# Twelve 64-column matmuls behind the second pair's scores, and a tensor_tensor in place of a tensor_scalar

## The chip, the core and the metric

The kernel runs on one core of a Trainium2 chip. The metric is the device time of one execution in microseconds (us), as a median of runs. TensorE (PE in the rows) multiplies matrices and writes to PSUM; VectorE (DVE), ScalarE (ACT) and GpSimd (POOL) work on elements; SyncE (SP) issues the DMA transfers. A matmul has its weights loaded by an instruction of its own (PEld in the rows).

## What is computed

An attention of 4 batches, 8 heads, 576 positions and 64 channels, half of the heads with a local mask of 32 positions and half with a mask of every 32nd position, is followed by four expert networks, each weighted by its share of domain_probs:

```python
def _attn_ref(q, k, v):
    scores = scale * np.matmul(q, k.transpose(0, 1, 3, 2))
    ...
    scores = np.where(masks[None, :, :, :], scores, -1000000000.0)
    scores = scores - np.max(scores, axis=-1, keepdims=True)
    attn = np.exp(scores)
    attn = attn / (np.sum(attn, axis=-1, keepdims=True) + 1e-09)
    return np.matmul(attn, v)

def _moe_ref(x, domain_probs, w1, w2):      # x: 2304 x 512
    p = domain_probs / (domain_probs.sum(-1, keepdims=True) + 1e-09)
    for e in range(4):
        h = np.maximum(x @ w1[e], 0.0)      # 512 x 1024
        out += p[:, e:e + 1] * (h @ w2[e])  # 1024 x 512
```

## The kernel before

**Stages.** Attention runs in 16 pairs (a batch and two heads each; "L" local, "S" strided). A pair's scores are small matmuls into PSUM banks named sc (L627 for L, L616 for S), VectorE adds the mask (L641), takes the maximum (L644) and the sum (L655); the subtraction (L647) and the norm (L659) go to VectorE or GpSimd, the exponential to ScalarE (L651). TensorE turns the weights (L706, L722, L739), they are copied out of PSUM (L526, L528), and products with v follow (L791, L771). The first 384 rows of the result are split into a high part xh (ScalarE, L849) and a low part xl (VectorE, L852), the others are copied to xr (L860, L862). Weights are split in the same way into a, s and w2t (high part L884 on ScalarE, low part L885 on VectorE or GpSimd), and each product is made of three passes, high by high, low by high and high by low. The first 384 rows go through all eight half experts by plain products (L969, L985) from about 18 to 198 us, woven with the rest of attention; after that the other rows go through in two parts by a recursive scheme with seven products in place of eight (L1155), with VectorE, ScalarE and GpSimd making the operands (a, s, ring, T, q).

**What sets the order.** Nothing is written in the order in which it runs. Every step is handed to a planner by `add(engine, duration, function, reads, writes, priority, ...)`, and `Plan.walk` plays the program through: for each engine it takes the step that can start first, with ties by priority, follows PSUM banks, the DMA queue and a model of TensorE's clock, and writes down an order in which the instructions are then issued. The durations are estimates in the code. A step marked "VP" goes to VectorE or GpSimd and one marked "AD" to ScalarE or VectorE, whichever the walk finds done first. A changed estimate can so move other steps and change engines. `fill` puts idle 512-column matmuls of a zero tile wz (L1526) into TensorE's early waits. A table SHIFT changes priorities of single steps by their number. Engines run their own instructions in order; waits are on semaphores, and a PSUM bank that TensorE writes is not read by VectorE before the writes to that bank that stand ahead are done.

**Names that come up.** raw are the loaded weights, 1 MB at a load (L874); prs are the domain probabilities, and `normalize` (L1462 to L1467) makes pr from them: a reduction into psums (L1463), the addition of 1e-9 (L1464), a reciprocal (L1465) and a product (L1466), all on VectorE. The second pair (n == 1) is a strided one; its scores are the 24 matmuls of L616 at about 9 us. q8 is the DMA queue by which an engine's instructions come.

Of the kernel before, what the change touches and what calls it, by code (L numbers as in the profile page):

```python
# [8 lines left out]
F32 = mybir.dt.float32  # L9
# [3 lines left out]
ALU = mybir.AluOpType  # L13
# [5 lines left out]
ZN = 30  # L19
# [371 lines left out]
def attn_moe_kernel(  # L391
# [14 lines left out]
    nc = tc.nc  # L406
    B, H, S, D = 4, 8, 576, 64
    NT, DM = B * S, out.shape[1]
    E, _, F = w1.shape
# [33 lines left out]
    psums = const.tile([P, NTT], F32, name="psums")  # L443
    wz = const.tile([P, 512], BF16, name="wz")
    warm = const.tile([P, 8], F32, name="warm")

    wt = {n: big.tile([P, 2, 2, 256], F32R, name=n) for n in QUART[:3] + ("s3",)}
    wq = {n: (t[:, 0], t[:, 1]) for n, t in wt.items()}
# [41 lines left out]
    KORD = (0, 2, 1, 3)  # L490
    JOIN = 4
    WHOLE = (1,)
    order = [(b, c) for b in range(B) for c in KORD]
    NP = len(order)
    plan = Plan(BANKS, MIX, tc)
# [44 lines left out]
    def plan_pair(n):  # L540
# [56 lines left out]
        for gi, (g0, g1) in enumerate(GRP[kd]):  # L597
# [11 lines left out]
            def scores(keys=keys, gi=gi, g0=g0, g1=g1, v0=0):  # L609
                ss = [bank(x) for x in keys]  # L610
                if kd == "S":
                    for o in range(0, 6 * W, W):
                        for x in range(2):
                            for h in range(2):
                                a = slice(64 * h, 64 * h + 64)
                                nc.tensor.matmul(  # L616
                                    ss[h][64 * x:64 * x + 64, o:o + W], qkv[a, x, o:o + 64],
                                    qkv[a, x, QKS + o:QKS + o + SR], start=True, stop=True)
                    return
                for r in range(3):  # L620
                    for v, s in enumerate(ss, v0):
                        for h in range(2):
                            for i in range(2):
                                a = slice(64 * h, 64 * h + 64)
                                t = QB * (2 * gi + v) + (96 * i + 32 * r if spans else 64 * r + 32 * i)
                                p = 64 * (h ^ v) + 32 * i
                                nc.tensor.matmul(  # L627
                                    s[p:p + 32, r * W:r * W + W], qkv[a, t:t + 32],
                                    qkv[a, t + 193:t + 193 + W], start=True, stop=True)
# [33 lines left out]
            dd = nel / 960 + 0.15  # L663
            vp = (dd, nel * 1.6e-3 + 0.22)
            if kd == "S" and gi == 0:
                add("PE", 0.88, scores, [f"qkS{bf}{i}" for i in range(2)], keys + [f"pmS{bf}{i}" for i in range(2)], z + 3, keys,
                    cols=4 * nel)
            elif n == 0 and gi == 0:
                for i, x in enumerate(keys):
                    add("PE", 0.46, half_scores(scores, x, i), [f"qkL{bf}0" + "ab"[i]], [x, tok], z + 3, x, cols=2 * nel)  # L670
            elif kd == "L":
                add("PE", (0.68, 0.46)[gi], scores, [f"qkL{bf}{gi}"], keys + [tok], z + 3, keys, cols=4 * nel)
# [103 lines left out]
        for gi in range(2):  # L776
# [65 lines left out]
            for (t0, nt, nm) in ((0, TA, "x"), (T0[1], TBS[0], "r1"), (T0[2], TBS[1], "r2")):  # L842
                for sel, cols in cut(t0, nt):
# [3 lines left out]
                    if nm == "x":  # L847
# [5 lines left out]
                                out=cols(xl[c]), in0=src(), in1=cols(xh[c].bitcast(F32)), op=ALU.subtract)  # L853

                        add("ACT", 0.42, xhi, [key], [f"xh{c}{g}"], z + 7.2)
                        add("DVE", 0.44, xlo, [key, f"xh{c}{g}"], [f"xl{c}{g}"], z + 7.4)
                    else:
                        def xraw(e, src=src, cols=cols, nm=nm):
                            if e == "ACT":
# [601 lines left out]

    def normalize():  # L1462
        nc.vector.tensor_reduce(out=psums, in_=prs, op=ALU.add, axis=AX.X)  # L1463
        nc.vector.tensor_scalar_add(out=psums, in0=psums, scalar1=1e-9)  # L1464
        nc.vector.reciprocal(out=psums, in_=psums)  # L1465
        nc.vector.tensor_tensor(  # L1466
            out=pr, in0=prs, in1=psums.unsqueeze(2).to_broadcast([P, NTT, E]), op=ALU.mult)  # L1467
# [5 lines left out]
        if n == 1:  # L1473
            add("POOL", 0.1, lambda: nc.gpsimd.memset(raws[2][:, 0, 0:1], 0.0), ["pmS00"], ["raw20", "raw21"], 0)
    add("SP", 0.4, load_pr, (), ["prs"], 8, xfer=((0.1, 128),))
    add("DVE", 1.0, normalize, ["prs"], ["pr"], ZN)
    key = ("ps", "pr")

    def turn_pr():
# [47 lines left out]

    with tc.manual_schedule():
        nc.vector.memset(wz, 0.0)
        make_identity(nc, ident)  # L1530
        for t in pm["S"]:
            nc.gpsimd.memset(t[:, :, SR + 1:64], 0.0)
# [87 lines left out]
```

## Time and profile before

| | |
|---|---|
| median of 3 runs | 778.45 us (776.25 to 778.79) |
| the profiled execution | 778.49 us |
| its span in the trace | 776.7 us |
| TensorE busy | 765.5 us, 5374 matmuls |
| VectorE busy | 620.8 us |
| ScalarE busy | 385.6 us |
| GpSimd busy | 206.4 us |

The span is what the trace covers, from the first instruction to the last. Busy TensorE time counts pipelined matmuls, so a busy stretch can still run at the lower clock; the granted clock (PEclk, 1.0 for 2.4 GHz and 0.5 for 1.2 GHz) tells that apart. Times in the rows are in us from the span's start.

### The profile page before, as it was taken

Reading aid. Unit: us, or ns where it says so; the run is one execution under the profiler, and the core shown is the slowest. Engines: PE = TensorE matmul, PEld = TensorE weight load, DVE = VectorE, ACT = ScalarE, POOL = GpSimd, SP = SyncE. Lnnn points to the kernel's source line nnn. Section 1 sums busy time; section 2 is a strip of 40 time slices with the busy share of each in tenths; the row PEclk is TensorE's granted clock in tenths of the full one; section 3 lists DMA queues with packets and bytes.
Section 4 is the critical chain, followed back from the end, with each engine's and each line's share of the span. In section 5 each row is a group of like instructions: output and inputs, shape, how many; then the busy total and the mean of one; then the engine's idle time right before and its main releaser. Section 6 shows DMA issues by size and latency. Waiting matters only on the chain.

```text
span 776.7 us, 14119 instructions
## 1 busy us (share of the span) xinstructions
PE 765.5 (99%) x5374; PEld 664.6 (86%) x5377; DVE 620.8 (80%) x1016; ACT 385.6 (50%) x726; POOL 206.4 (27%) x198
## 2 busy tenths in 40 slices
PE   7999999999999999999999999999999999999997
PEld 4788888889989999999999998888888888888886
DVE  6877777798698897889798997758765976599895
ACT  4635544474566375646727654644354344523330
POOL 5412011012131522454373264001000330033250
PEclk9999999999999999999999999999999999999999
DMA  9999999778899798899989838955665697659624
GB/s 321 305 394 380 339 326 353 276 252 327 311 388 343 257 359 288 328 237 350 350 254 275 272 119 221 395 207 220 236 265 198 193 215 288 232 173 247 215 82 162
DMA packets 89630, 212.67 MB, mean 274 GB/s; under 512 B 7071, under 2 KB 33883, under 8 KB 89563
## 3 DMA queue, kind: packets, MB, share of 16 engines
q1 hardware_dynamic: 83659, 201.96, 71.8%
q0 software_dynamic: 5760, 9.70, 7.9%
q8 instruction: 42, 0.69, 0.3%
q10 hardware_dynamic: 144, 0.11, 0.1%
q14 instruction: 25, 0.20, 0.1%
HBM read 138.58 MB, written 73.17 MB: 273 GB/s over the span
## 4 chain that ended last, share of the span: by engine, by line
PE 95%; DVE 2%; DMA 1%; ACT 1%; issue 1%; POOL 0%; DVEq 0%; ACTq 0%
PE mo L1155 26%; PE ps L1155 25%; PE sc L1155 20%; PE mo L985 9%; PE mo L969 9%; PE ps L771 2%; DMA ring<-d27a 1%; PE sc L627 1%; PE ps L739 1%; PE sc L616 1%; PE mo L1526 1%; PE ps L791 0%; ACT q L1207 0%; DVE w2t L885 0%; DVE pmL L641 0%
## 5 line engine op out<-in xcount | busy, mean ns | idle before, releaser
L1155 PE MATMUL sc<-T,ring 128*128 128x448 f32 (+2 forms) x774 | 174.3, 374 | 0.0
L1155 PEld LDWEIGHTS sc<-T,ring 128*128 128x128 f32 x774 | 144.5, 188 | 19.7
L1240 ACT ACTIVATE T<-q 128x512 fp32r<-128x512 f32 (+1 forms) x196 | 112.6, 601 | 69.0 <-PE mo L1155 26.4
L1242 DVE TENSOR_TENSOR T<-q,T 128x512 fp32r<-128x512 f32 (+1 forms) x152 | 104.7, 703 | 15.9 <-ACT T L1240 15.2
L1203 DVE TENSOR_TENSOR q<-ps,v 128x448 f32<-128x448 f32 (+1 forms) x96 | 62.5, 654 | 35.3 <-PE ps L1155 30.9
L1155 PE MATMUL mo<-T,ring 128*128 128x512 f32 (+1 forms) x396 | 90.0, 376 | 0.0
L1207 ACT ACTIVATE q<-q 128x448 f32<-128x448 f32 (+1 forms) x84 | 49.9, 598 | 71.7 <-DVE q L1203 70.8
L1155 PEld LDWEIGHTS mo<-T,ring 128*128 128x128 f32 x396 | 74.3, 188 | 10.3
L1242 POOL TENSOR_TENSOR T<-q,T 128x448 fp32r<-128x448 f32 (+1 forms) x44 | 53.1, 1215 | 91.8 <-ACT T L1240 69.9
L985 PE MATMUL mo<-w2t,hs 128*128 128x512 f32 x288 | 71.2, 397 | 0.0
L1194 ACT ACTIVATE v<-mo 128x448 f32<-128x448 f32 (+1 forms) x96 | 54.5, 567 | 25.7 <-PE mo L1155 25.0
L1352 DVE TENSOR_TENSOR acc<-sc,acc 128x512 f32<-128x512 f32 (+1 forms) x85 | 54.9, 654 | 13.9 <-PE sc L1155 13.1
L1284 POOL TENSOR_TENSOR q<-q,q 128x512 f32<-128x512 f32 (+1 forms) x12 | 15.4, 1284 | 181.5 <-DVE T L1242 164.9
L985 PEld LDWEIGHTS mo<-w2t,hs 128*128 128x128 f32 x288 | 52.7, 188 | 11.0
L1284 DVE TENSOR_TENSOR q<-q,q 128x448 f32<-128x448 f32 (+1 forms) x88 | 58.9, 681 | 2.5 <-POOL T L1242 1.4
L526 ACT ACTIVATE acc<-sc 128x448 f32<-128x448 f32 (+1 forms) x41 | 23.2, 567 | 48.5 <-PE sc L1155 46.9
L969 PE MATMUL mo<-xh,a 128*128 128x384 f32 x192 | 45.7, 341 | 0.0
L1352 DVE TENSOR_TENSOR acc<-mo,acc 128x512 f32<-128x512 f32 (+1 forms) x52 | 34.0, 658 | 14.0 <-PE mo L1155 11.3
L1155 PE MATMUL ps<-T,ring 128*128 128x448 f32 (+1 forms) x180 | 40.8, 375 | 0.5 <-DMA ring<-d27a 0.5
L1155 PEld LDWEIGHTS ps<-T,ring 128*128 128x128 f32 x180 | 33.7, 188 | 5.3 <-DVE acc L1352 0.8
L1155 PE MATMUL ps<-t4h,a 128*128 128x448 f32 (+1 forms) x128 | 35.2, 376 | 0.2 <-DVE q L1203 0.2
L1155 PE MATMUL ps<-t3h,s 128*128 128x448 f32 (+1 forms) x128 | 35.2, 376 | 0.1
(179 smaller groups left out, 1437.6 us busy)
## 6 DMA issues: line engine op xcount, KB each, us to landing
raw<-in_w SPq DMA_DIRECT2D x28, 1024.0 KB, 8.3
qkS<-in_qk_strided SPq DMA_DIRECT2D x16, 329.0 KB, 8.2
vstL<-in_v_local SPq DMA_DIRECT2D x6, 640.0 KB, 9.7
po<-acc POOLq DMA_DIRECT2D x16, 224.0 KB, 7.2
vstS<-in_v_strided SPq DMA_DIRECT2D x8, 384.0 KB, 7.8
a<-d16a SPq DMA_DIRECT2D x6, 512.0 KB, 8.7
ring<-d27a SPq DMA_DIRECT2D x6, 512.0 KB, 6.5
a<-d10a SPq DMA_DIRECT2D x6, 512.0 KB, 4.7
```

Source lines behind the costliest of these rows:

```text
L526: nc.scalar.activation(out=dst(), in_=src(held[key]), func=AF.Copy)
L771: nc.tensor.matmul(oo[hf][64 * h:64 * h + 64, o:o + w], a, pt[r, x, c0:c0 + w], start=True, stop=True)
L969: nc.tensor.matmul(pt[:, 0:TA], w[:, c % 2, (f % 2) * P:(f % 2) * P + P], (xl if i == 1 else xh)[c], start=j == 0, stop=j == 11)
L985: nc.tensor.matmul(pt, ht[f][:, ts], wt[f][:, cs], start=j == 0, stop=j == 11)
L1155: nc.tensor.matmul(pt, a[i == 2][:, j, f * P:f * P + P], skewed(b[i == 1][j], TH)[:, cs], start=bool(first) and n == 0, stop=True, skip_gr ...
L1194: add("ACT", TH / 1200 + 0.18, lambda: nc.scalar.activation(out=late["u"][i][:, 0:TH], in_=held[key][:, 0:TH], func=AF.Copy), [key, "late2 ...
L1203: add("DVE", DD, lambda: nc.vector.tensor_tensor(out=q(), in0=src(), in1=late["u"][i][:, 0:TH], op=ALU.add), [key, f"u{i}", "late2"], [tok ...
L1207: add("ACT", TH / 1200 + 0.2, lambda: nc.scalar.activation(out=q(), in_=q(), func=AF.Relu), ["late2"], [tok], zs)
L1240: add("ACT", TH / 1200 + 0.17, lambda src=src, hi=hi: nc.scalar.activation(out=hi(), in_=src(), func=AF.Copy), [tok, "late2"], [f"T{i}h{j} ...
L1242: add("VP", vp, lambda e, src=src, hi=hi, lo=lo: engine(e).tensor_tensor(out=lo(), in0=src(), in1=hi().bitcast(F32), op=ALU.subtract), [to ...
L1284: add("VP", vp, lambda e, d=d, x=x, y=y: engine(e).tensor_tensor(out=d[0](), in0=x[0](), in1=y[0](), op=ALU.subtract), [x[1], y[1]], [d[1] ...
L1352: add("DVE", DD, lambda av=av, key=key: nc.vector.tensor_tensor(out=av(), in0=held[key][:, 0:TH], in1=av(), op=ALU.add), [key], tok, zd)
```

## The change

Behind the 24 score matmuls of the second pair, twelve matmuls with zero weights wz and 64 columns of wz are written into a free part of the pair's first score bank (columns 324 to 387; nothing reads them). The planner is told of them by a longer duration and more columns for that step. The addition of 1e-9 to the domain sums becomes a tensor_tensor with a tile tiny, set to 1e-9 at the start by VectorE, and its planned duration goes from 1.0 to 0.85 for the four operations; the planned duration of each xl goes from 0.44 to 0.54.

```diff
+    tiny = const.tile([P, NTT], F32, name="tiny")
...
+    PAD = 12
...
+                    for _ in range(PAD if n == 1 else 0):
+                        nc.tensor.matmul(ss[0][:, 6 * W:6 * W + 64], wz[:, 0:P], wz[:, 0:64], start=True, stop=True)
...
-                add("PE", 0.88, scores, [f"qkS{bf}{i}" for i in range(2)], keys + [f"pmS{bf}{i}" for i in range(2)], z + 3, keys,
-                    cols=4 * nel)
+                add("PE", 0.88 + (PAD * 0.03 if n == 1 else 0), scores, [f"qkS{bf}{i}" for i in range(2)], keys + [f"pmS{bf}{i}" for i in range(2)], z + 3, keys,
+                    cols=4 * nel + (PAD * 64 if n == 1 else 0))
...
-                        add("DVE", 0.44, xlo, [key, f"xh{c}{g}"], [f"xl{c}{g}"], z + 7.4)
+                        add("DVE", 0.54, xlo, [key, f"xh{c}{g}"], [f"xl{c}{g}"], z + 7.4)
...
-        nc.vector.tensor_scalar_add(out=psums, in0=psums, scalar1=1e-9)
+        nc.vector.tensor_tensor(out=psums, in0=psums, in1=tiny, op=ALU.add)
...
-    add("DVE", 1.0, normalize, ["prs"], ["pr"], ZN)
+    add("DVE", 0.85, normalize, ["prs"], ["pr"], ZN)
...
         nc.vector.memset(wz, 0.0)
+        nc.vector.memset(tiny, 1e-9)
```

Lines move down by one to five in the changed file (L616 becomes L618, the new matmuls are L622, L1464 becomes L1468). By the programs' lists TensorE gets 24 instructions more (12 loads and 12 matmuls), VectorE goes from 1018 to 1024 operations, GpSimd from 203 to 197, ScalarE from 729 to 730; SyncE keeps its 395.

TensorE at the second pair's scores, at about 9 to 14 us, before:

```order
L1526 MATMUL mo<-wz 128x512
L616 MATMUL sc<-qkS_263 64x54 x24
L706 MATMUL ps<-ident,pmL_269 128x128 x6
L1526 LDWEIGHTS wz
L1526 MATMUL mo<-wz 128x512
L627 MATMUL sc<-qkL_261 32x63 x12
L627 MATMUL sc<-qkL_262 32x63 x12
L791 MATMUL ps<-pTL,vstL_265 64x96 x8
```

and now, with ten of the twelve equal pairs left out:

```order
L1530 MATMUL mo<-wz 128x512
L618 MATMUL sc<-qkS_264 64x54 x24
L622 LDWEIGHTS wz
L622 MATMUL sc<-wz 128x64
...
L622 LDWEIGHTS wz
L622 MATMUL sc<-wz 128x64
L710 MATMUL ps<-ident,pmL_270 128x128 x6
```

The pads stand between the scores and the turning of the first pair's weights. Behind them TensorE's order is the same up to about 38 us, 24 instructions further back.

VectorE around the domain sums, at about 28 to 36 us, before (numbers behind names are buffers):

```order
L659 TENSOR_TENSOR pmS_272<-pmS_272,sm 128x6x54
L885 TENSOR_TENSOR w2t<-raw_226,w2t 128x512
L1463 TENSOR_REDUCE psums<-prs 128x18
L1464 TENSOR_SCALAR psums<-psums 128x18
L1465 RECIPROCAL psums<-psums 128x18
L1466 TENSOR_TENSOR pr<-prs,psums 128x72
L641 TENSOR_TENSOR pmL_269<-sc,both 128x3x63 x2
L885 TENSOR_TENSOR w2t<-raw_226,w2t 128x512 x2
L862 COPY xr_241<-ps 128x6x6x3
L852 TENSOR_TENSOR xl_249<-ps,xh_245 128x6x12x3
L885 TENSOR_TENSOR a_77<-raw_225,a_77 128x512
L852 TENSOR_TENSOR xl_249<-ps,xh_245 128x6x12x3
```

and now:

```order
L889 TENSOR_TENSOR w2t<-raw_227,w2t 128x512
L1467 TENSOR_REDUCE psums<-prs 128x18
L1468 TENSOR_TENSOR psums<-psums,tiny 128x18
L1469 RECIPROCAL psums<-psums 128x18
L1470 TENSOR_TENSOR pr<-prs,psums 128x72
L530 COPY pTS<-ps 128x6x64
L651 TENSOR_TENSOR pmL_270<-pmL_270,mx 128x9x63
L856 TENSOR_TENSOR xl_250<-ps,xh_246 128x6x12x3
L645 TENSOR_TENSOR pmL_271<-sc,both 128x3x63
L889 TENSOR_TENSOR a_78<-raw_226,a_78 128x512
L856 TENSOR_TENSOR xl_250<-ps,xh_246 128x6x12x3
```

The norm of pmS and a w2t have left VectorE here, a copy of pTS and a subtraction of pmL have come, and a mask stands ahead of the a between the two halves of xl.

GpSimd at the same time, before:

```order
L885 TENSOR_TENSOR w2t<-raw_226,w2t 128x512
L647 TENSOR_TENSOR pmL_269<-pmL_269,mx 128x9x63
L885 TENSOR_TENSOR s_80<-raw_225,s_80 128x512
L659 TENSOR_TENSOR pmL_269<-pmL_269,sm 128x9x63
L647 TENSOR_TENSOR pmS_271<-pmS_271,mx 128x12x54
```

and now:

```order
L663 TENSOR_TENSOR pmS_273<-pmS_273,sm 128x6x54
L889 TENSOR_TENSOR w2t<-raw_227,w2t 128x512 x2
L889 TENSOR_TENSOR s_81<-raw_226,s_81 128x512
L889 TENSOR_TENSOR w2t<-raw_227,w2t 128x512
L889 TENSOR_TENSOR a_79<-raw_226,a_79 128x512
```

The low part of s follows two w2t directly, with no subtraction of pmL ahead of it. Further differences of this kind lie on all engines up to about 230 us; on SyncE they lie at about 200 to 230 us only.

## Rows read from the trace of the kernel before

**Rows 1.** The page's head and part 1: busy us (share) xinstructions of each engine.

```profile
span 776.7 us, 14119 instructions
PE 765.5 (99%) x5374; PEld 664.6 (86%) x5377; DVE 620.8 (80%) x1016; ACT 385.6 (50%) x726; POOL 206.4 (27%) x198
```

**Rows 2.** TensorE's waits, whole span: us in total, times, longest.

```profile
PE ps L771 <- issue: 1.4, 1, 1.4
```

**Rows 3.** TensorE's waits from 36.2 us to the end.

```profile
PE mo L969 <- DVE xl L852: 0.5, 1, 0.5
PE ps L1155 <- DMA ring<-d27a: 0.5, 1, 0.5
PE ps L1155 <- DVE q L1203: 0.2, 1, 0.2
```

**Rows 4.** By stretches: length, busy of PE, PEld, DVE, ACT, POOL, PEclk, DMA, GB/s.

```profile
23.00:24.00 1.00, 0.86 (x16) 0.80 (x16) 0.00 (x0) 0.38 (x2) 0.18 (x1) 0.82 1.01 407
24.00:25.00 1.00, 1.00 (x27) 0.56 (x33) 0.60 (x2) 0.75 (x4) 0.00 (x0) 0.50 1.04 407
...
27.00:28.00 1.00, 1.00 (x9) 0.94 (x8) 0.30 (x1) 0.83 (x2) 0.00 (x0) 0.97 1.03 360
```

**Rows 5.** Timeline, TensorE at the standstill: start, us, what, idle before and its end.

```profile
20.54 0.33 PE L969 MATMUL mo<-xl,s 128*128 128x384 f32 x1
...
20.98 0.78 PE L771 MATMUL ps<-pTS,vstS 54*64 54x54 f32 x34
23.14 0.45 PE L771 MATMUL ps<-pTS,vstS 54*64 54x54 f32 x14 [1.38 <-issue]
...
23.92 0.52 PE L969 MATMUL mo<-xl,s 128*128 128x384 f32 x1
```

**Rows 6.** The page's part 3, queue of instructions: packets, MB, share.

```profile
q8 instruction: 42, 0.69, 0.3%
```

**Rows 7.** The DMA view from 20 to 21 us: packets, MB, share by queue.

```profile
q1 hardware_dynamic: 175, 0.34, 109.4%
q8 instruction: 1, 0.02, 10.3%
```

**Rows 8.** Timeline from 10 to 30 us: around the pads' place.

```profile
10.75 0.88 DVE L641 TENSOR_TENSOR pmS<-sc,both 128x324 f32<-128x324 f32 x2
...
10.97 0.85 PE L706 MATMUL ps<-ident,pmL 128*128 128x128 f32 x6 [0.99 <-DVE pmL L659]
...
11.55 0.10 PEld L1526 LDWEIGHTS <-wz 128*128 128x128 bf16 x1
...
13.62 0.88 PE L791 MATMUL ps<-pTL,vstL 128*64 128x96 f32 x16 [0.79 <-ACT pmS L651]
...
15.72 0.38 SPq L874 DMA_DIRECT2D raw<-in_w  x1
...
29.12 0.59 PE L739 MATMUL ps<-ident,pmS 64*128 64x64 f32 x12
```

**Rows 9.** Timeline from 24 to 37 us, VectorE, GpSimd and TensorE in turn.

```profile
24.40 0.55 DVE L852 TENSOR_TENSOR xl<-ps,xh 128x216 fp32r<-128x216 f32 x1 [1.87 <-ACT xr L860]
27.70 0.56 DVE L852 TENSOR_TENSOR xl<-ps,xh 128x384 fp32r<-128x384 f32 x1 [0.96 <-ACT xh L849]
28.58 0.69 DVE L885 TENSOR_TENSOR w2t<-raw,w2t 128x512 fp32r<-128x512 f32 x1
29.44 1.10 DVE L1464 TENSOR_SCALAR psums<-psums 128x18 f32<-128x18 f32 x1
34.43 1.21 DVE L885 TENSOR_TENSOR a<-raw,a 128x512 fp32r<-128x512 f32 x1
...
29.22 1.28 POOL L885 TENSOR_TENSOR w2t<-raw,w2t 128x512 fp32r<-128x512 f32 x1 [2.63 <-issue]
33.95 1.14 POOL L647 TENSOR_TENSOR pmL<-pmL,mx 128x567 f32<-128x567 f32 x1 [3.45 <-DVE mx L644]
35.05 1.73 POOL L885 TENSOR_TENSOR s<-raw,s 128x512 fp32r<-128x512 f32 x1
...
36.16 0.44 PE L969 MATMUL mo<-xl,a 128*128 128x384 f32 x1 [0.52 <-DVE xl L852]
```

## The prediction

> **What bounds the kernel now.** I read the share of the engines first [rows 1]: TensorE is busy for 765.5 of 776.7 us. The end moves only where TensorE stands still or runs at its lower clock. The list of its waits names 1.4 us before matmuls of L771, put down to "issue", which means that the profile shows nothing waited for [rows 2]; from 36.2 us to the end there are three, 1.2 us together [rows 3]. Before about 21 us it waits more, but there VectorE sets the pace and such waits do no harm by themselves. The view by stretches [rows 4] shows a second loss: after the standstill the granted clock falls to 0.50, the 1.2 GHz level, from within the row 23:24 to within the row 27:28. The shares of those two rows (0.36 and 0.06 us at half) and the three microseconds between them make 3.4 us at half speed; a matmul of L969 took 0.52 us there and 0.33 before [rows 5]. Half of 3.4, **1.7 us**, is lost. With the standstill's 1.38 us [rows 5] that is 3.1 us in one place, 0.4% of the time.
>
> The profiled execution took 778.49 us, 1.8 more than its span. The median of the three runs is 778.45, so a sum made against this execution holds against the median. One of the three took 776.25, 2.2 less, about the size of this loss; whether it is this loss the runs do not say. A measurement of this kernel can tell about 0.3% (2.3 us) from no change.
>
> **The standstill.** The instruction queue q8 moved 42 packets with 0.69 MB [rows 6], 16.4 KB each; TensorE has 5374 + 5377 instructions [rows 1], so a packet is 256 of them. One lies in the microsecond from 20 to 21, with the DMA share at about one [rows 7], just before TensorE stops at the 34th of 48 matmuls of L771 [rows 5]. So I read the standstill as code that comes late. Counting 256 TensorE instructions (matmuls, loads, waits) back along the timeline leads into the L791 group at 13.62 [rows 8]. If the packet was asked for there, it moved 7 us later, behind other traffic and after the 1 MB load of raw issued at 15.72 [rows 8].
>
> The Trainium skill, "Runtime: NRT & Kernel Launch", section "Instruction fetch mechanics", says that code is fetched ahead in blocks of 256 instructions and that this is mostly hidden. By that sentence the standstill would have another cause and would stay, which is the second rival below; the row with the packet speaks against it.
>
> **The twelve matmuls.** They stand behind L616 of the second pair, where TensorE waits 0.99 us for VectorE until 10.97 [rows 8]. The trace has no row of their form. Nearest from below: transposes of 64 columns, 12 in 0.59 us (L739). Nearest from above: one load of wz, 0.10 us, if every load stays in the open, 12 x 0.10 = 1.2 us [rows 8]. I take 0.8, nearer the transposes, since loads run beside matmuls. That lies inside the 0.99 us: cost 0, at most 0.25. VectorE's second mask of this pair now waits for them too; it begins at about 11.2 (10.75 and half of 0.88, [rows 8]), late enough for pads of up to 1.2 us.
>
> Their other effect is that everything later in TensorE's program stands 24 instructions further back, so each border between code blocks comes 24 instructions earlier in the work. The place 256 before the standstill moves from L791, which TensorE enters at 13.62 after a 0.79 us wait, to matmuls of L627 ahead of that wait, some 1.2 us sooner and further ahead of the raw load. Bounds for the standstill: nothing left, or 1.6 us (it is met 12 small matmuls, 0.2 us, earlier and the packet is no sooner). I take **0.3 us left, -1.1**, nearer to nothing, because a request that stands in front of raw has less to wait behind. L969 would then fill the time before the row 23:24 in which the clock fell, and I expect it to hold: **-1.7**. Its bounds are 0 and 1.7.
>
> **The domain sums.** The tensor_scalar took 1.10 us for 18 columns, where 512 columns of w2t take 0.69; it ran from 29.44 to just behind the end of GpSimd's w2t (29.22 to 30.50) [rows 9]. As a 0.2 us operation it would give VectorE 0.9. But VectorE's two-input a<-raw,a at 34.43 took 1.21 and ended 0.55 behind GpSimd's 33.95 to 35.09 [rows 9]. So the tensor_tensor, or the two-input pr behind it, can wait for w2t just as long: gain 0 to 0.9. I take 0.3, nearer to none, since GpSimd has two w2t in a row there now. The memset of tiny comes behind that of wz, while VectorE waits for the first scores: 0.
>
> The skill, "SBUF — State Buffer", section "Who interferes with whom", says that a VectorE instruction with two SBUF inputs contends with a GpSimd one that reads SBUF, and the later one waits in full. The a<-raw row agrees. By the rule the swap alone gives VectorE 0, by the plain duration 0.9, and the sum below would be 776.4 or 775.5.
>
> **The new plan.** The changed durations and costs reorder work from about 28 to 230 us; behind that all engines' orders are those of before. On VectorE's way to its last xl the order loses the norm of pmS, a w2t and a copy of xr, and gains a copy of pTS, a subtraction of pmL and a mask. Those are operations of 0.3 to 0.7 us (as w2t and a mask in [rows 8, 9]): three against three, taken as 0, within 0.7. DMA orders change only at some 200 us. The same loads stand ahead of the ring load that TensorE waits 0.5 us for [rows 3]: 0, between -0.5 and +0.7.
>
> **The sum.** TensorE would reach the L969 that now starts at 36.16 behind xl [rows 9] 1.1 + 1.7 = 2.8 us sooner, at 33.4. VectorE's two idle waits before it, 1.87 and 0.96 us [rows 9], are for copies of TensorE's results: the first shrinks by 1.1, the second goes, so xl comes 2.1 sooner, 2.4 with the 0.3 of the sums. TensorE still waits there, and the **2.4 us** of VectorE are what is left: 778.5 - 2.4 = **776.1 us**. From there TensorE is back to back and carries it to the end.
>
> **The rivals.**
> - *The code comes earlier and the clock falls all the same.* For it: the clock fell after this standstill in the one execution that I see, and idle stretches before 17 us did not lower it, so what decides is not in the rows. Then -1.1, of which VectorE gives back 0.3: 777.7.
> - *The change does not do what it says.* The packet moves when the DMA queue lets it, and the pads fill an idle 0.99 us and nothing more. Then 778.5, within 0.5.
> - *VectorE gets late (slower).* GpSimd's low part of s, which came behind pmL at 35.05 [rows 9], now follows w2t directly. If it starts at about 35.0, when ScalarE has its high part, and VectorE's a, now behind a mask that needs TensorE's L627, comes after that, a waits for some 1.3 us (as w2t's 1.28, [rows 9]) and xl ends 1.2 later: 779.7. It decides when VectorE's a comes after 35.0, that is if the standstill stays. And it can repeat: six operations leave GpSimd (203 to 197) for VectorE, at some 0.65 us; with no cover 3.9, 782.4. Against it: TensorE waits for nothing between 37 and 230 us, so there is slack. The middle is 780.3, two thirds of the way being the repeats.
>
> **How the numbers follow.** Forecast (776.1, own range 774.8 to 777.4) 0.55; the clock falls 0.15; no effect 0.12; VectorE late 0.18. Below 776.1 lie half of the first, 0.28, and 0.02 of the second and third with a ring wait that vanishes: faster 0.30. Above 780.8 lie two thirds of the last, since a first lateness tends to be followed by others: slower 0.13. Within 0.3% is the rest, 0.57. For 8 in 10 the range runs from 774.8, the forecast's own low end, to 780.3, which leaves out the worse part of the slow case.
>
> **What would show it.** The standstill in L771 under 0.6 us; a granted clock of 1.0 in every row from 20 to 30; L706 starting at 11.0 or little later with the pads before it; the psums operation at 0.2 us, or at about 1 with a GpSimd operation that ends with it; the L969 behind xl at about 33.8 instead of 36.16; no new TensorE waits from 37 to 230. I am wrong if the packet still comes at 20.6 and the clock falls, or if TensorE waits for VectorE by more than 1 us in the stretch to 190 us.

## The result, and the profile after

The changed kernel takes 783.71 us (783.56 to 784.70, 6 runs) where the kernel before takes 777.34 (776.21 to 778.79, 6 runs with the three known earlier): a ratio of 1.0085, with a 95% interval from 1.0069 to 1.0100. It is slower by 6.4 us. I had forecast 776.1 and at most 780.3.

The first thing to see is that several steps of the forecast came true in the trace and were still worth nothing. The profile of the changed kernel by stretches (length, busy of PE, PEld, DVE, ACT and POOL, granted clock, DMA share, GB/s), which answers to [rows 4]:

```profile
23.00:24.00 1.00, 1.00 (x51) 0.70 (x49) 0.44 (x1) 0.89 (x3) 0.34 (x1) 1.00 1.04 409
24.00:25.00 1.00, 0.96 (x27) 0.69 (x16) 0.95 (x4) 0.56 (x1) 0.13 (x1) 1.00 1.03 387
...
27.00:28.00 1.00, 1.00 (x17) 0.68 (x15) 0.97 (x3) 1.00 (x2) 0.87 (x1) 1.00 0.75 219
```

The clock held at 1.0. The twelve matmuls took 0.52 us in the trace (10.00 to 10.52), inside the wait that was there. The standstill within the group of strided products, 1.38 us in [rows 5], is 0.35 in its row now:

```profile
21.23 0.56 PE L775 MATMUL ps<-pTS,vstS 54*64 54x54 f32 x23
22.14 0.61 PE L775 MATMUL ps<-pTS,vstS 54*64 54x54 f32 x25 [0.35 <-issue]
```

This shorter standstill says little by itself: over all traces of this case it is 0.0 to 1.0 us in the seven with the shift of 24 and 0.5 to 1.4 in the eleven without.

And yet the page's first lines show a span 6.2 us longer, with TensorE busy for 4.6 us more with the twelve matmuls as its only new work [rows 1]:

```profile
span 782.9 us, 14145 instructions
...
PE 770.1 (98%) x5386; PEld 664.5 (85%) x5389; DVE 625.4 (80%) x1022; ACT 385.2 (49%) x727; POOL 197.9 (25%) x192
```

TensorE's waits, which answer to [rows 2, 3]: the one for xl grew from 0.5 to 1.4, the one for ring from 0.5 to 0.9, and "issue" stands in two groups:

```profile
PE mo L973 <- DVE xl L856: 1.4, 1, 1.4
...
PE ps L775 <- issue: 1.2, 2, 0.8
PE ps L1159 <- DMA ring<-d27a: 0.9, 1, 0.9
PE sc L631 <- issue: 0.7, 1, 0.7
```

The 0.8 of L775 lies at 136 us, where TensorE did not stand still before; the 0.7 of L631 lies at 13 us. VectorE and GpSimd on the way to that xl, which answer to [rows 9] (start, duration):

```profile
26.25 1.01 DVE L889 TENSOR_TENSOR w2t<-raw,w2t 128x512 fp32r<-128x512 f32 x1
...
27.43 1.02 DVE L1468 TENSOR_TENSOR psums<-psums,tiny 128x18 f32<-128x18 f32 x1
...
28.78 0.97 DVE L1470 TENSOR_TENSOR pr<-prs,psums 128x72 f32<-128x72 f32 x1
...
34.05 1.78 DVE L889 TENSOR_TENSOR a<-raw,a 128x512 fp32r<-128x512 f32 x1
35.76 0.52 DVE L856 TENSOR_TENSOR xl<-ps,xh 128x216 fp32r<-128x216 f32 x1
...
27.13 2.53 POOL L889 TENSOR_TENSOR w2t<-raw,w2t 128x512 fp32r<-128x512 f32 x2 [0.42 <-POOL pmS L663]
34.02 1.28 POOL L889 TENSOR_TENSOR s<-raw,s 128x512 fp32r<-128x512 f32 x1 [4.36 <-ACT s L888]
```

Before, the last xl had begun at 35.56:

```profile
35.56 0.54 DVE L852 TENSOR_TENSOR xl<-ps,xh 128x216 fp32r<-128x216 f32 x1
```

The two-input operations end behind GpSimd's: psums, pr and a take 1.02, 0.97 and 1.78 us, and xl begins at 35.76, 0.2 later than before. Whatever TensorE won by 30 us is gone there.

That explains the start, not the 4.6 us of busy time. Longer matmuls stand in the large products, behind 198 us. The groups of TensorE by shape (busy us, mean ns of one), first three of the kernel before, then of the changed one:

```profile
L1155 PE MATMUL ps<-b11h,a 128*128 128x512 f32 x64 | 18.4, 389 | 0.0
...
L1155 PE MATMUL ps<-t2h,s 128*128 128x512 f32 x64 | 18.4, 389 | 0.0
...
L1155 PE MATMUL ps<-b11h,a 128*128 128x448 f32 x64 | 16.7, 362 | 0.0
```

```profile
L1159 PE MATMUL sc<-T,ring 128*128 128x512 f32 x378 | 90.9, 389 | 0.0
...
L1159 PE MATMUL ps<-t3h,s 128*128 128x512 f32 x64 | 18.9, 396 | 0.0
L1159 PE MATMUL ps<-b11h,a 128*128 128x512 f32 x64 | 18.8, 396 | 0.0
...
L1159 PE MATMUL mo<-t1h,s 128*128 128x512 f32 x64 | 18.6, 392 | 0.0
...
L1159 PE MATMUL ps<-t2h,s 128*128 128x512 f32 x64 | 18.4, 389 | 0.0
...
L1159 PE MATMUL ps<-b11h,a 128*128 128x448 f32 x64 | 17.0, 366 | 0.0
```

The same instruction with the same shapes takes 395 or 396 ns in place of 389 in the high groups of b11, b21, t3 and t4; not in t2 nor in T by ring. Over these four products with 512 columns (64 matmuls by 5 to 7 ns in each of the high groups, 32 by 6 to 9 in each of the low ones) and 448 columns (3 to 4 ns each) that is 4.0 us; t1 and b22 are longer too, by less (392 and 391 ns), which adds 0.4. (The busy time of before also holds the 1.7 us of the lower clock, so these do not add up to the 4.6.) What sets the four apart is not in the program's order but in its memory. Their weight tiles a11, a12, a22 and s3 are allocated at the low end of SBUF behind the constants, their moving tiles b and t at the high end. The compiled programs, from which these addresses are, place tiles at multiples of 32 bytes, so tiny (72 bytes) takes 96:

```
byte within a partition         before   changed
tiny                                 -      4256
a11 (weights of b11)              4768      4864
T0 / ring0 (one product)   53920/123552  54016/123648
b11h0 (moving)                  153504    153504
s2 / t2h0 (one product)   214944/186272  214944/186272
```

T and ring moved together, s2 and t2 not at all; a11 and b11 moved apart by 96 bytes. No row of the profile before shows an address.

### The profile page after: what moved, and what is told of

The parts are those of the page before. It is cut to its first block, busy times and chain, and to the rows that moved or that the text cites. A ratio compares the mean times of both kernels' runs of the same rounds, so it can differ in the third digit from the quotient of the medians.

```text
span 782.9 us, 14145 instructions
## 1 busy us (share of the span) xinstructions
PE 770.1 (98%) x5386; PEld 664.5 (85%) x5389; DVE 625.4 (80%) x1022; ACT 385.2 (49%) x727; POOL 197.9 (25%) x192
## 4 chain that ended last, share of the span: by engine, by line
PE 94%; DVE 2%; DMA 1%; ACT 1%; issue 1%; POOL 0%; DVEq 0%; POOLq 0%
PE mo L1159 26%; PE ps L1159 26%; PE sc L1159 20%; PE mo L989 9%; PE mo L973 8%; PE ps L775 2%; DMA ring<-d27a 1%; PE sc L631 1%; PE sc L618 1%; PE ps L743 1%; PE mo L1530 1%; DVE xl L856 0%; ACT q L1211 0%; DVE mx L648 0%; DVE a L889 0%
## 5 line engine op out<-in xcount | busy, mean ns | idle before, releaser
L1288 DVE TENSOR_TENSOR q<-q,q 128x448 f32<-128x448 f32 (+1 forms) x88 | 57.3, 663 | 4.0 <-POOL T L1246 2.5
```

Source lines behind the costliest of these rows:

```text
L1288: add("VP", vp, lambda e, d=d, x=x, y=y: engine(e).tensor_tensor(out=d[0](), in0=x[0](), in1=y[0](), op=ALU.subtract), [x[1], y[1]], [d[1] ...
```

## The experiments

Every time stands beside runs of the kernel before on the same chip.

### Where the tiles stand

**A dead tile in tiny's place**, in the kernel before:

```diff
     warm = const.tile([P, 8], F32, name="warm")
+    dead = const.tile([P, 18], F32, name="dead")
```

> The kernel before with one edit: a tile of 18 floats per partition that nothing reads or writes, allocated where tiny stands. Tiles are placed at multiples of 32 bytes, so it takes 96 bytes, and a11, a12, a22, s3, the T and ring tiles move up by 96; the b, t, s1, s2 and s4 tiles at the other end of SBUF stay. Program order and instructions are those of before. Theory A (placement: a product is slower when its stationary and its moving tile no longer stand alike): the 512-column products of b11, b21, t3 and t4 take 395 to 398 ns in place of 389, those with 448 columns 365 to 368 in place of 362, T by ring stays at 389; TensorE busy about 4.6 us more; time 782.0 (781.3 to 782.7). Theory B (the longer matmuls come from the new order, from the twelve added ones or from what other engines do): everything as before, 777.3.

Measured: 781.50 us against 777.31, ratio 1.0065 (1.0041 to 1.0090). A tile that nothing touches costs 4.2 us. The same groups are longer, by the same amounts:

```profile
L1156 PE MATMUL ps<-t3h,s 128*128 128x512 f32 x64 | 18.9, 396 | 0.0
L1156 PE MATMUL ps<-b11h,a 128*128 128x512 f32 x64 | 18.8, 396 | 0.0
```

**Which distance?** Three more shifts: the changed kernel with tiny made 128 bytes wide, the kernel before with a dead tile of 64 bytes, and the kernel before with the tiles at the high end moved by 32.

```diff
-    tiny = const.tile([P, NTT], F32, name="tiny")
+    tiny = const.tile([P, 32], F32, name="tiny")[:, 0:NTT]
```

> The changed kernel with tiny made 32 floats wide (128 bytes; only the first 18 are used), so that everything above it moves by 128 bytes and no longer by 96; all else as changed. Theory A (placement, by the place within 64 or 128 bytes): all 512-column products at 389 ns and 448-column ones at 362 again, TensorE busy about 4.6 us less than in the changed kernel, time 783.7 - 4.6 = 779.1 (778.3 to 779.9): still 1.8 above before, for what the early stretch lost. Theory B: products at 395 as in the changed kernel, 783.7.

Measured: 785.70 us against 777.31, ratio 1.0106 (1.0090 to 1.0123). My first idea, the place within 64 or 128 bytes, fell: b11h stayed at 394 ns. That this is 2.0 us more than the changed kernel took goes with the clock: in three of the four executions the mean granted clock is 0.998, and the profiled one shows where it fell, to 0.50 (the 1.2 GHz level) for 3.4 us from 37.5 us on, just behind a wait of 1.5 us for xl:

```profile
36.90 0.45 PE L973 MATMUL mo<-xl,a 128*128 128x384 f32 x1 [1.49 <-DVE xl L856]
```

```profile
37.00:38.00 1.00, 1.00 (x5) 1.00 (x6) 0.97 (x3) 0.45 (x1) 0.00 (x0) 0.74 1.05 369
38.00:39.00 1.00, 1.00 (x5) 1.00 (x4) 0.97 (x3) 0.53 (x2) 0.00 (x0) 0.50 1.11 389
```

```diff
+    dead = const.tile([P, 16], F32, name="dead")
```

> The kernel before with a dead tile of 16 floats (64 bytes) in the place of tiny. If what counts is the place within 64 bytes: 512-column products of b11, b21, t3 and t4 stay at 389 ns, time 777.3 within 1.3. If it is the place within 128 bytes or more, or the bare fact that two tiles have moved against each other: 395 ns or more, 782. Theory B: 389, 777.3.

Measured: 781.25 us in one run, 394 to 396 ns for the four products. So it is not the place within 64 bytes.

```diff
             tmp["s", i] = p.tile([P, 2, 256], F32, name=f"tmp{i}")
+        p.tile([P, 8], F32, name="dead")
```

> The kernel before with a dead tile of 8 floats (32 bytes) behind the tmp tiles at the other end of SBUF, which moves b11 to t4, s1, s2 and s4 down by 32 bytes, onto multiples of 64; a11, a12, a22, s3, T and ring stay 32 above one. If the two tiles of a product must stand alike within 64 bytes: b11, b21, t3, t4 at 395 ns and t1, t2, b22 (whose s1, s2, s4 move with them) at 389, time about 782. If it is that a stationary tile on a multiple of 64 is bad for a moving one that is not (the case of the changed kernel alone): all at 389, 777.3. Theory B: 389, 777.3.

Measured: 783.42 us in one run, the four products at 395 and 396 ns. Here a11 stayed and b11 moved, in dead96 the other way round: it is the distance that counts and not the place of either tile. It need not be the distance of a matmul's own two tiles alone: t1 and b22, whose two tiles moved together or not at all, take 391 to 393 ns in all these runs (high groups, 512 columns), t2 389 or 390. What the products between which they run have to do with it was not tested. Of the products with 512 columns all distances of before are multiples of 256 (a11 to b11: 581 times 256), which gives the next test:

```diff
+    dead = const.tile([P, 64], F32, name="dead")
```

> The kernel before with a dead tile of 64 floats (256 bytes) where tiny stands. In the kernel before, the two tiles of every product stand apart by a multiple of 256 bytes (a11 and b11 by 148736, T and ring by 0 within 2048), and shifts by 64, 96 and 128 bytes and one by 32 the other way all made them slower. Theory A256 (they must stand apart by a multiple of 256): all 512-column products back at 389 ns, time that of before, 777.3 within 0.9. Theory A-other (the exact distance of before is what is good, or any move of a against b hurts): b11, b21, t3, t4 at 395 ns or more, 781.5.

Measured: 777.08 us against 777.14, ratio 1.0002 (0.9990 to 1.0014). All groups are back, t1 and b22 too:

```profile
L1156 PE MATMUL ps<-t3h,s 128*128 128x512 f32 x64 | 18.4, 389 | 0.0
...
L1156 PE MATMUL ps<-b11h,a 128*128 128x512 f32 x64 | 18.4, 389 | 0.0
```

The same in the changed kernel, with `tiny = const.tile([P, 64], F32, name="tiny")[:, 0:NTT]`:

> The changed kernel with tiny 64 floats wide (256 bytes, 18 floats used). Theory A256: products at 389 and 362 ns again, TensorE busy some 4.6 us less than in the changed kernel, time 783.7 - 4.6 = 779.1 (778.2 to 780.0). What is left above 777.3 is what the changed kernel's trace shows ahead of 250 us: the wait for xl 0.9 longer, a standstill of 1.0 at 136 us, the ring wait 0.4 longer, less the 0.9 by which it led at 34 us. Theory A-other: 783.7 or more.

Measured: 780.99 us against 777.14, ratio 1.0050 (1.0034 to 1.0065), with 389 ns in all these groups. The rest of the slowdown, 3.9 us, is more than the 1.8 that I expected to be left. Part of it is the clock again: four of the six executions have a mean granted clock of 0.997 or 0.998 (780.74 to 782.31), two of 1.0 (779.42 and 780.20), 2.7 above before.

### The new order

The four planning numbers of the changed kernel in the kernel before, without the twelve matmuls and without tiny. Of the four, the two for the twelve matmuls leave every engine's planned order as it was (no run has them alone); the two VectorE durations make the new order.

```diff
-                        add("DVE", 0.44, xlo, ...
+                        add("DVE", 0.54, xlo, ...
...
-    add("DVE", 1.0, normalize, ["prs"], ["pr"], ZN)
+    add("DVE", 0.85, normalize, ["prs"], ["pr"], ZN)
```

> The kernel before with the four planning numbers of the changed kernel and nothing else: order as changed (the cost of the twelve matmuls alone leaves the order as it was, so the two VectorE durations make the difference), no twelve matmuls, no tiny, SBUF as before. Theory R (the new order is dear by itself: VectorE's last xl before TensorE's wait at 36 us comes nearly 3 us later than in the old order, because w2t, pr and a wait for GpSimd and a copy, a subtraction and a mask stand before it): 779.8 to 781.0, with a wait for xl of over 1 us at 34 to 36 us. Theory T (it is dear only together with the twelve matmuls, through the place of the code blocks): 777.2 within 0.8.

Measured: 780.77 us against 776.86, ratio 1.0047 (1.0034 to 1.0060). Estimates in the code, which no instruction uses, cost 3.9 us. The median hides two kinds of execution: 779.39 and 779.98 with a granted clock of 0.999 and 1.0, some 2.8 above before, and 780.77 to 781.49 with 0.997 or 0.998. In the kernel before, run beside it, none of 23 is under 0.999. So some 2.8 of the 3.9 are the order's waits, and the rest goes with a clock that falls more often in this order. TensorE's waits show the same places as the changed kernel:

```profile
PE ps L771 <- issue: 1.7, 2, 1.0
PE mo L969 <- DVE xl L852: 1.5, 1, 1.5
...
PE ps L1155 <- DMA ring<-d27a: 1.1, 1, 1.1
```

Each of the two alone, the first hunk of that diff and then the second:

> The kernel before with the planned duration of the xl subtraction at 0.54 in place of 0.44, nothing else. VectorE then has a mask of the next pair ahead of its last xl there, and a<-raw,a before both, as in the changed kernel, but a copy of xr on VectorE still. Theory R1 (this number brings the dear order): most of what planonly costs, 779 to 781. Theory R2 (it takes both): 777.1 within 0.8.

> The kernel before with the planned duration of normalize at 0.85 in place of 1.0, nothing else. VectorE then does its xl ahead of the maximum of pmL, and the a<-raw,a between the last two xl is gone from VectorE's way. Theory R1 (the xl number brings the dear order): 777.1 within 0.8, or less than before, down to 775.5, where the wait for xl shortens. Theory R3 (this number brings it): 779 to 781.

Measured: 778.25 us (ratio 1.0016, 1.0007 to 1.0024) and 778.38 (1.0021, 1.0013 to 1.0030). Neither brings the dear order alone; both orders are a little worse than the old one.

**What is dear in it?** The order of planonly, with three GpSimd subtractions (two w2t at 27 us, one s at 34 us) replaced by a memset of the same tile:

```diff
+        def low(e):
+            if e == "POOL":
+                gone[0] += 1
+                if gone[0] in (3, 4, 5):
+                    nc.gpsimd.memset(lo().bitcast(F32), 0.0)
+                    return
+            engine(e).tensor_tensor(out=lo(), in0=src(), in1=hi().bitcast(F32), op=ALU.subtract)
```

> The order of planonly, with three GpSimd operations replaced, the two w2t at 27 us and the low part of s at 34 us: each writes zeros over the same tile in place of subtracting (so these low parts are left out of the computation). They then read nothing from SBUF. Theory X (the new order is dear because VectorE's two-input operations there wait for GpSimd's: w2t 0.33, the sum 0.79, pr 0.73, a 0.93 us longer than where GpSimd is idle): those four at 0.69, 0.2, 0.23 and 0.82 us, xl some 2 to 2.8 us sooner, TensorE's wait for it from 1.95 to about 0.3; time 1.0 to 2.0 under planonly, so 1.9 to 2.9 above before. Theory Y (the operations that VectorE gained are what is dear): wait over 1.5, time as planonly, 3.9 above before.

Measured: 777.44 us against 777.00, ratio 1.0000 (0.9986 to 1.0015). Nothing clear of the noise is left of the 3.9, in the order of planonly with nothing changed but these three. That is 3.3 under planonly, more than the 1.0 to 2.0 of theory X; part of it is the clock, which is at 0.999 or 1.0 in all eleven executions. GpSimd's memsets, VectorE's operations there, and TensorE's waits:

```profile
26.85 0.99 POOL L891 MEMSET w2t<- 128x512 f32 x2
32.95 0.53 POOL L891 MEMSET s<- 128x512 f32 x1 [5.11 <-PE mo L978]
```

```profile
27.63 0.24 DVE L1473 TENSOR_SCALAR psums<-psums 128x18 f32<-128x18 f32 x1
...
28.20 0.23 DVE L1475 TENSOR_TENSOR pr<-prs,psums 128x72 f32<-128x72 f32 x1
...
33.72 0.68 DVE L893 TENSOR_TENSOR a<-raw,a 128x512 fp32r<-128x512 f32 x1
34.32 0.53 DVE L852 TENSOR_TENSOR xl<-ps,xh 128x216 fp32r<-128x216 f32 x1
```

```profile
PE ps L771 <- issue: 1.2, 2, 0.7
...
PE mo L978 <- DVE xl L852: 0.4, 1, 0.4
...
PE ps L1164 <- DMA ring<-d27a: 0.2, 1, 0.2
```

psums takes 0.24 where planonly has 1.01, pr 0.23 for 0.96, a 0.68 for 1.75: without GpSimd's three subtractions VectorE does not wait and the price of the new order is gone. Two things stay open. The memsets are shorter as well (0.5 us each where a subtraction takes 1.3) and end before pr and a begin, so the run does not tell reading from length. And the waits for xl (1.5 to 0.4) account for 1.1 us of that only; the ring wait (1.1 to 0.2) and the standstills (1.7 to 1.2) shrank too, and that these follow from the same cause is not shown. The operations that VectorE gained are still there (1021 in both traces, 1016 before). Counted from the xl at about 26 us to the last one, VectorE takes 7.7 us in the old order (dead256), 10.0 in planonly and 8.3 here: the gained operations put xl 0.6 later, of which nothing shows in the total.

### The domain sums

```diff
-        nc.vector.tensor_scalar_add(out=psums, in0=psums, scalar1=1e-9)
+        nc.vector.tensor_tensor(out=psums, in0=psums, in1=tiny, op=ALU.add)
```

alone, with tiny 256 bytes wide and the old order:

> The kernel before with the tensor_tensor for the domain sums alone, tiny made 256 bytes wide so that the products keep their distances, order as before. The tensor_scalar took 1.10 us beside a GpSimd w2t. Theory Z (the tensor_tensor waits for it as long): about 1.0 us, time of before within 0.7. Theory Z2 (it does not wait): 0.2 us, xl 0.8 sooner, time 0.3 to 0.7 under before.

Measured: 776.95 us against 777.00, ratio 0.9999 (0.9990 to 1.0008). VectorE's sum and GpSimd's operation beside it:

```profile
27.83 1.00 DVE L1465 TENSOR_TENSOR psums<-psums,tiny 128x18 f32<-128x18 f32 x1
```

```profile
27.45 1.34 POOL L886 TENSOR_TENSOR w2t<-raw,w2t 128x512 fp32r<-128x512 f32 x1 [1.39 <-issue]
```

It ends just behind w2t, as the tensor_scalar did [rows 9]. The swap changes nothing that can be measured.

### The twelve matmuls

Alone, in the kernel before, with costs and order as they were:

```diff
+                    for _ in range(PAD if n == 1 else 0):
+                        nc.tensor.matmul(ss[0][:, 6 * W:6 * W + 64], wz[:, 0:P], wz[:, 0:64], start=True, stop=True)
```

> The kernel before with the twelve matmuls alone: no tiny, no change to the sums, costs and order of before, so nothing moves in SBUF. Theory P (my forecast's account of the pads: a shorter standstill, a clock that holds, carried to the end as far as VectorE lets it): 775.2 (774.5 to 776.2). Theory Q (the late code block only stands in another place, and what is won before 30 us ends in a longer wait for xl): 777.3 (776.4 to 778.2), with the granted clock at 1.0 through 20 to 30 us or not.

Measured: 778.31 us against 777.14, ratio 1.0017 (1.0008 to 1.0026). They lose a little, and the waits say where: besides the old standstill there are two new ones behind 30 us, in L794 (0.7 us, at 33) and in L630 (0.7, at 77). The 0.8 of L630 lies at 13 us, where VectorE sets the pace.

```profile
PE sc L630 <- issue: 1.5, 2, 0.8
...
PE ps L774 <- issue: 1.0, 1, 1.0
...
PE ps L794 <- issue: 0.7, 1, 0.7
```

I then did what the forecast had not: I followed every border between blocks of 256 TensorE instructions through the trace of a kernel in the old order (dead256), from the standstill on, and read how long each block lasts. In the old order the shortest ones last 4.9 us (30.0 to 34.8) and 5.7 us (72.4 to 78.1). Borders 24 instructions earlier fall into stretches of small attention matmuls, and the two blocks last 3.2 us (29.8 to 33.1) and 4.4 us (72.2 to 76.5), which I took to be too short for the next one to arrive. The two new standstills begin in the matmul groups where these borders lie, and in the DMA view a q8 packet moves shortly before each, in the microseconds 31:32 and 75:76. Two more runs test that. The twelve at the very front, in TensorE's first idle time:

```diff
         for _ in range(n):
             nc.tensor.matmul(t, wz[:, 0:P], wz, start=True, stop=True)
+        for _ in range(0 if held.get("front") else 12):
+            nc.tensor.matmul(t[:, 0:64], wz[:, 0:P], wz[:, 0:64], start=True, stop=True)
+        held["front"] = True
```

> The kernel before with the same twelve small matmuls put behind the very first warm-up matmuls on TensorE, where it waits for its first data, and not behind the scores of the second pair. Everything later stands 24 TensorE instructions further back, as with the twelve in their place. Theory U (the 1.2 us of the twelve alone come from where the borders of 256 instructions fall: with a shift of 24 two blocks are used up in 3.2 us, at 30 to 33, and 4.4 us, at 72 to 77, before 4.9 and 5.7): as padsonly, 1.2 above before (0.6 to 1.8), with standstills at about 33 and 77 us. Theory V (the twelve disturb VectorE's mask and TensorE where they stand): as before, within 0.5.

Measured: 779.90 us against 777.00, ratio 1.0032 (1.0020 to 1.0045): 2.9 above, more than the 1.8 at most of my bounds, with the standstills in L791 (1.5 us, at 34) and L627 (1.0, at 79) where the borders say, and longer than in padsonly (the 0.9 left of L627 lies at 13 us):

```profile
PE sc L627 <- issue: 1.8, 2, 1.0
PE ps L791 <- issue: 1.5, 1, 1.5
...
PE ps L771 <- issue: 1.0, 1, 1.0
```

Three matmuls in place of twelve, a shift of 6 (`PAD = 3`):

> The kernel before with three small matmuls in place of twelve, behind the scores of the second pair: a shift of 6 instructions. Theory U: the two blocks last 4.4 and 5.2 us, between those of before (4.9, 5.7) and of the twelve (3.2, 4.4), so the standstills at 33 and 77 us go or shrink: 0 to 0.6 above before. Theory V: a quarter of the twelve's cost, 0.3 above before. Theory W (any shift costs the same): 1.2 above.

Measured: 777.09 us against 777.00, ratio 1.0002 (0.9993 to 1.0011), and no standstill at 33 or 77 us; one of 0.6 us, at 86 us, does not show in the time (right32, without any of these matmuls, has one of 0.8 there). So it is where the borders fall, not the work of the twelve.

The length of a block does not decide alone. In the changed kernel, whose order is another, two borders with the shift of 24 also lie behind short blocks (30.5 to 34.0 and 74.5 to 78.5, 3.5 and 4.0 us), and TensorE goes on there without a stop; the packet for the second one moves in 74:75, over 3 us ahead. And the standstill at 136 us, which planonly has without the twelve (0.7 us), ends a block of about 5 us. When a packet moves counts as well, and what sets that is not shown.

### The parts together

The twelve matmuls and the tensor_tensor with the old order and the old distances (the four planning numbers put back, tiny of 256 bytes):

> The changed kernel with tiny of 256 bytes and with the four planning numbers of before, so that the order on all engines is that of before: the twelve matmuls and the tensor_tensor are left. Theory R (the new order is what costs the rest: VectorE's pr, w2t and a wait for GpSimd, the code block late at 136 us): as padsonly within 0.5, and 1.5 to 3 under after256. Theory S (the tensor_tensor or the pads cost it): as after256, 779.1.

Measured: 778.14 us against 777.14, ratio 1.0015 (1.0005 to 1.0024): as the twelve alone, and 2.9 under the changed kernel with the old distances. The changed kernel once more:

> The changed kernel once more, so that its parts are compared beside the same runs of before: if the parts add (place of the tiles 4.6, new order 2.9, twelve matmuls 1.2, tensor_tensor 0), 777.1 + 8.6 = 785.7, of which the early slack may hide some: 783.5 to 786. If they hide each other, 783.5 or under.

Measured: 784.71 us against 776.86, ratio 1.0098 (1.0085 to 1.0111), 7.9 us above. The distances (4.2 by dead96) and the new order (3.9 by planonly) make 8.1. Here two of the four executions are at a granted clock of 1.0, 783.70 and 784.13, and in the 6.4 of the result all six are at 0.999 or 1.0; against these the order counts with its 2.8 at the full clock, 7.0 together where 6.4 to 7.3 was measured. In the new order the twelve add nothing more: planonly and after256, without and with them, are 3.9 and 3.9 above before, and 2.8 and 2.7 at the full clock.

## Why the prediction was wrong

**The price of tiny.** I costed its memset, at 0, by the work that hides it, and did not ask what the tile itself moves. That step was missing, and it was the largest: 4.2 us by dead96, of 6.4 to 7.9. The code had a hint that I read past: the kernel before holds a dead tile `skew1` of 64 bytes among the late tiles and a function `skewed` that starts narrow moving tiles 64 bytes into their slot. Both only make sense where the place of a tile counts.

**"Three against three, taken as 0, within 0.7."** The new order costs 3.9, some 2.8 of it at the full clock. The operations themselves were rightly priced: poolset, where the waits are gone, has xl 0.6 later than the old order. But I counted VectorE's operations at the durations that they have while GpSimd is idle, and a sentence of my own, two paragraphs earlier, should have stopped me: GpSimd has two w2t in a row there now. Their waits, 1.7 us by poolset, are the term that was missing.

The mechanism stood in the prediction as the third rival: a behind GpSimd's s waits some 1.3 us. That came: a took 1.78 where poolset gives 0.68. What was wrong was the condition and so the chance, 0.18. I let it decide only "if the standstill stays", with s at a fixed 35.0. That was misread: s then waited for GpSimd's pmL, which is gone from there in the new order, while ScalarE's high part was done at 34.6. With TensorE early, ScalarE was 0.7 earlier still, before and now:

```profile
33.97 0.63 ACT L884 ACTIVATE s<-raw 128x512 fp32r<-128x512 f32 x1
```

```profile
33.27 0.61 ACT L888 ACTIVATE s<-raw 128x512 fp32r<-128x512 f32 x1
```

So s began at 34.02 and met a at 34.05. In a chain that moves as a whole, a collision moves with it. The rival's second part, 3.9 for operations that leave GpSimd for VectorE, did not come: five of the six go to VectorE and one to ScalarE (1021 against 1016, 727 against 726 in planonly), and poolset has them all without loss. That the new order also measures 3.9 is luck.

**The domain sums, -0.3.** The bounds were 0 and 0.9 and the end at 0 was right: 1.00 us in ttonly for 1.10 before.

The Trainium skill, "SBUF — State Buffer", section "Who interferes with whom", says that a VectorE operation with two SBUF inputs and a GpSimd one that reads SBUF do not run side by side, the later waits in full. The runs agree that the later one waits: with two SBUF inputs psums ends just behind w2t (1.00 us in ttonly). But the tensor_scalar, with one, waited as long (1.01 in planonly), so the second input is not what makes the difference here; and whether a GpSimd operation that only writes stands in the way no run here shows, since poolset's memsets were nearly or wholly over when VectorE's operations began.

**The twelve matmuls, -1.1.** The step was that the border moves from L791 to matmuls of L627 and the packet comes sooner. For that one border it holds in part: 1.0 us of standstill with the twelve alone (padsonly), 1.1 without (ttonly and dead256 have 1.1 in their waits, less than the 1.4 of the execution that I forecast from). Over all traces the spread from execution to execution is as large as the gain that I forecast. And a shift moves all borders behind it, and I looked at one. Two others fell where, by dead256's trace, a block lasts 3.2 and 4.4 us; the twelve alone lose 1.2 us. The Trainium skill, "Runtime: NRT & Kernel Launch", section "Instruction fetch mechanics", has code fetched ahead by blocks of 256, mostly hidden. The 256 agrees with the borders found here; that it is mostly hidden holds for most blocks and not for these.

**The clock, -1.7.** It held, as forecast, and that was worth nothing to the median, because it was no property of the kernel. Profiles of other kernels with the old order, dead256 and ttonly, show a granted clock of 1.0 in the same stretch, and medians equal to the kernel before. Of dead256:

```profile
23.00:24.00 1.00, 1.00 (x51) 0.75 (x50) 0.37 (x1) 0.96 (x3) 0.00 (x0) 1.00 1.04 255
24.00:25.00 1.00, 0.95 (x30) 0.71 (x18) 0.97 (x4) 0.56 (x1) 0.05 (x1) 1.00 0.78 221
```

The size of the term was right: this execution took 776.69, 1.8 less than the one from which I forecast. What was wrong was to credit it to the change. Of 86 executions of the kernel before on four chips, five have a mean granted clock of 0.998 or less.

The prediction noticed that one of three runs was 2.2 us shorter, "about the size of this loss", and then built on the longer execution all the same. In 29 other runs of the kernel before the median is 777.1: a base that I had set 1.3 too high.

**The sum** left 2.4 us of gain, what VectorE's way to the last xl would give back. That limit was right as a thought and too generous: xl was the place where the early gain was lost, TensorE's wait for it growing from 0.5 to 1.4, and the matmul behind it began at 36.34, where I had 33.8 and before it was 36.16.

## What to carry to other kernels

A new tile is an edit to every address behind it: before adding one, look which products have their two operands on either side of it, and keep their distance (here a tile of 256 bytes in place of 96 gives the 4 us back). Two-input VectorE work is costed with what GpSimd does at that moment, and a collision is looked for again after everything has moved. Of one profiled execution, what differs from run to run is no gain to forecast: compare its time with the spread first, and the granted clock of each execution, since a median of few runs can be one with the lower clock.

## What the runs showed of the hardware

- **A matmul's time depends on how the SBUF tiles of the products lie to each other.** With 512 columns, in the high groups of the four products: 389 or 390 ns at the distances of before and when these changed by 256 bytes, 394 to 396 ns when they changed by 64, 96 or 128 bytes or by 32 the other way (393 to 400 in the low groups). With 448 columns, whose moving tiles start 64 bytes further in, 362 to 365 and 364 to 370. All this is with the same instructions (dead96, dead64, right32, dead256; for 128 bytes the changed kernel's after128). Why is not shown; that the matmul's own read and the load of the next weights meet in SBUF is a guess. The Trainium skill, "SBUF — State Buffer", section "Who interferes with whom", gives TensorE two independent reads, one for the moving tile and one for weights, and says that it waits for no one. For waits on other engines nothing here speaks against that; but these two reads, if they are what meets, are not independent, and 4 us hang on it.
- **Code can come late more than once, and a shift of 24 instructions early on changes where.** Standstills of 0.6 to 1.5 us came in the old order at borders at about 33 and 77 us, with the DMA share at 0.8 to 1.1 there (padsonly, padsfront, noplan256), and none with a shift of 6 (pads3). Short blocks alone are no rule: the changed kernel passed two of 3.5 and 4.0 us without a stop.
- **What makes the clock fall stays open.** In profiled executions it fell after a standstill of 1.38 us (before) and after a wait of 1.49 us for xl (after128), and not after waits of 1.39 to 1.51 us for the same xl in the changed kernel, after_again, after256 and planonly, nor after the 1.1 us of dead256. It is met more often where that wait is long: the mean granted clock is 0.998 or less in 11 of 25 executions of the kernels with the new order and GpSimd's subtractions in place (after, after_again, after128, after256, planonly), in 5 of 86 of the kernel before and in none of 11 of poolset.
